# Half-height matmul tiles for the folding and the numerators, constant rows copied by DMA, and a new table of offsets

## The chip, the core and the metric

The kernel runs on one core of a Trainium2 chip. The metric is the time of the whole program on the device, in microseconds (us), as the median of several runs. TensorE (PE) does the matmuls and loads their weights, VectorE (DVE), ScalarE (ACT) and GpSimd (POOL) do the elementwise work, and SyncE (SP) issues all DMAs of this kernel, in order, from one queue.

## What is computed

Two attention layers over 2048 tokens of width 1024, with 32 heads of 32, are computed and set side by side. Layer A is causal softmax attention within four segments plus a compressive memory across them. Layer B is linear attention with a learned feature map. The change touches three places: the constants of A's score product, the product of B's per-head matrix `w_phi` with its projection weights (folding), and B's numerators.

```python
def _B_ref(x, wqkv, w_phi, wo):
    qkv = (x @ wqkv) -> q, k, v of [heads 32, tokens 2048, 32]
    pq = jnp.einsum("bhsd,hdf->bhsf", q, w_phi)      # folded: (wqkv, w_phi) before x
    pk = jnp.einsum("bhsd,hdf->bhsf", k, w_phi)
    phi_q = jnp.concatenate([_softmax(pq), _softmax(-pq)], axis=-1)   # 64 features a head
    phi_k = jnp.concatenate([_softmax(pk), _softmax(-pk)], axis=-1)
    kv = jnp.einsum("bhsf,bhsd->bhfd", phi_k, v)     # 64 x 32 a head
    z = jnp.einsum("bhsf->bhf", phi_k)
    num = jnp.einsum("bhqf,bhfd->bhqd", phi_q, kv)   # the numerators
    den = jnp.einsum("bhqf,bhf->bhq", phi_q, z)[..., None] + 1e-6
    return (num / den -> [tokens, 1024]) @ wo
```

## The kernel before

Nothing is issued in the order in which it is written. The code records operations (`op(engine, duration, function, reads, writes, priority)`) in a graph; `Graph.run` then plays the engines forward with the durations written down for each operation and, whenever an engine is free, issues the ready operation of least priority number. The table `MOVES` adds an offset to the priority, by engine and by the running number of the job (a stretch of operations of equal priority). PSUM has eight banks; `Graph.bank` gives them out by kind (`proj`, `s`, `misc`, `pv`, `kv`), and `KEEP` and `MOST` say how many a kind may hold. Numbers are kept in f32 and multiplied as pairs of f16 halves, three products for each (high by high, high by low, low by high), except in the folding, which is an f32 matmul.

The program has four stages.

- **Start** (to about 20 us). Thirty-two f32 matmuls of an identity (L1195) run on PE while the first weights and the first segment land. ACT measures the sum of the absolute weights (L469), PE spreads it over the partitions (L405), DVE measures the segment (L463), and both are split into halves (L415 to L429). The first product (L394) needs all of that. Tiles `S12` to `S14` (`stk`) hold queries and keys; their partitions 96 to 103 carry a constant that the score product (L971) uses, written by three ACT operations (L651).
- **Layer A** (to about 917 us). For each of 32 units, `produce` makes queries, keys and values and `attend` the scores, exponentials and sums. One `fold` stands in each unit: it loads a 128x512 block of `wqkv` (`st`), multiplies its four 128x128 pieces by a 128x128 matrix that has four heads' `w_phi` on its diagonal (`phib`), L1112, into one `misc` bank, and DVE scales the bank into `quad` (L1115).
- **Layer B, keys and values, then queries** (to about 1531 us). `strassen` (L608) makes the products with `x`. For each of 16 token blocks c and each half hb of the heads, POOL, DVE and ACT make the features and their halves, a DMA transposes them into `pt` (L1603), and the numerators follow (L1612): 24 matmuls, each with a 128x64 weight tile (two heads, their 64x32 matrices on the diagonal, the rest zero) and 128 moving columns, into the 64 upper or the 64 lower partitions of a `pv` bank. ACT (L1616) and DVE (L1618) take the bank into the halves of `ot`, and `project` (L394, `misc<-S,ot`) multiplies by B's output weights.
- **Layer A's output product** (L1666, to the end).

The folding and the numerators are these lines.

```python
for c in range(4):
    op(PE, 0.22, lambda c=c: nc.tensor.matmul(ps()[:, c, :], st()[:, c * 128:(c + 1) * 128], phib()[:, g, :], ...
...
for g in range(4):
    for a, b in ((0, 0), (0, 1), (1, 0)):
        for k in range(2):
            nc.tensor.matmul(pn()[64 * k:64 * k + 64, g, :], kls()[:, a, 8 * hb + 2 * g + k, :], pt()[:, b, 2 * g + k, :], ...
```

Of the kernel before, what the change touches and what calls it, by code (L numbers as in the profile page):

```python
# [12 lines left out]
AF = mybir.ActivationFunctionType  # L13
OP = mybir.AluOpType
# [5 lines left out]
D = 1024  # L20
# [41 lines left out]
    "ACT": {  # L62
# [9 lines left out]
    "POOL": {  # L72
        67: 17, 70: -1, 93: -6, 131: -0.5, 141: 1, 148: -7.5, 199: 13.5, 217: -4, 238: -38, 245: 0.5, 250: -4.5, 312: -5},
    "SP": {
        88: 5.5, 89: 3.5, 134: 33.5, 149: -3.5, 226: -19.5},
# [23 lines left out]
class Graph:  # L99
# [84 lines left out]
    def run(self):  # L184
# [15 lines left out]
        def bank(kind):  # L200
            rest = [x for x in banks if x[1] is None]
            if used[kind] >= self.MOST[kind] or len(rest) <= sum(
                    max(0, n - used[k]) for k, n in self.KEEP.items() if k != kind):
                return never, None
            return min((x[0], i) for i, x in enumerate(banks) if x[1] is None)

        def start(o):
            t = max(o.ready, held["POOL" if o.eng == "DVE" else "DVE"]) if o.port else o.ready
            for b in o.banks:
                if b.at is None:  # L210
                    t = max(t, bank(b.kind)[0])
            return t

        def safe(o):

            return max([o.safe] + [bank(b.kind)[0] + self.SLACK for b in o.banks if b.at is None])

        count = 0
        for _ in self.ops:
# [16 lines left out]
            n = 0  # L236
# [43 lines left out]
def tile_kernel(ctx: ExitStack, tc: tile.TileContext, ax, aw, awv, awo, beta, bx, bwqk, bwv, bphi, bwo, out):  # L280
# [369 lines left out]
    for t in stk:  # L650
        op(ACT, 2.0, lambda t=t: nc.scalar.activation(t()[96:104, 1], sel[96:104, :, None].to_broadcast([8, 4, 512]), AF.Copy),  # L651
           w=[(t, (1, 3))], prio=0.3)
# [420 lines left out]
    def fold(n, prio, dep=()):  # L1073
# [36 lines left out]
        ps = bank("misc", [128, 4, 128], "fold")  # L1110
        for c in range(4):
            op(PE, 0.22, lambda c=c: nc.tensor.matmul(ps()[:, c, :], st()[:, c * 128:(c + 1) * 128], phib()[:, g, :],  # L1112
                                                      start=True, stop=True), r=[st, phib], w=[ps], prio=prio, need=[qd])
        k = 2 * q + hb
        op(DVE, 0.62, lambda: nc.vector.tensor_scalar(qd()[:, k], ps().rearrange("p c n -> p (c n)"), si()[:, 1:2], None, op0=OP.mult),  # L1115
# [622 lines left out]
```

## Time and profile before

| | |
|---|---|
| median of 3 runs | 1698.13 us (1698.09 to 1698.71) |
| profiled execution | 1699.08 us, its span 1697.4 us |
| mean granted TensorE clock | 0.994 of full |
| PE busy | 1668.2 us (98%) |
| DVE, ACT, POOL busy | 1354.2, 1158.9, 965.4 us |

The span is the time from the first to the last instruction; 1.68 us of the profiled execution lie around it. PE is busy nearly throughout, so an engine other than PE matters where PE waits for it, and a microsecond of PE's own work counts in full where PE does not wait. Matmuls are pipelined: a row's duration reaches from the first matmul's start to the last one's end, while the pace is the distance from start to start.

### The profile page before, as it was taken

The page shows a single profiled execution, that of the slowest core. Times are in us where ns is not written, and L with a number is a line of the kernel's source. Part 1 is how long each engine was busy: PE and PEld are TensorE (multiplying, and loading weights), DVE is VectorE, ACT ScalarE, POOL GpSimd, SP SyncE. Part 2 cuts the span into 40 slices and gives each one's busy share as a digit, 9 for nine tenths or more (in the row PEclk, how much of TensorE's full clock was granted, in tenths as well). Part 3 has the DMA queues.
Part 4 walks back from the last instruction along what each step waited for, and adds up shares of the span by engine and source line. Part 5 has one row for each costly group of instructions (what it writes and reads, how often), then busy time and mean ns, then how long its engine had stood idle before and what let it go on. Part 6 is the DMA issues. An engine that isn't in the chain of part 4 may idle for free.

```text
span 1697.4 us, 38668 instructions
## 1 busy us (share of the span) xinstructions
PE 1668.2 (98%) x14408; PEld 1002.5 (59%) x14408; DVE 1354.2 (80%) x3205; ACT 1158.9 (68%) x2131; POOL 965.4 (57%) x1280
## 2 busy tenths in 40 slices
PE   8999999999999999999999999999999999999999
PEld 6677676766767767767765455445544444444444
DVE  5889998899988869698895779677998887975441
ACT  8788899878879797868675477765545644544331
POOL 3346588554468885848552577645488887640000
PEclk8999999999999999999999999999999999999999
DMA  5556465755776665764467465467645876773311
GB/s 192 165 183 176 139 206 175 242 160 163 225 179 204 184 173 150 199 189 131 95 182 266 156 224 162 137 194 278 224 94 149 199 162 174 214 168 129 124 62 62
DMA packets 261933, 292.47 MB, mean 172 GB/s; under 512 B 138865, under 2 KB 192881, under 8 KB 255089
## 3 DMA queue, kind: packets, MB, share of 16 engines
q1 hardware_dynamic: 261744, 290.01, 57.3%
q8 instruction: 113, 1.85, 0.5%
q14 instruction: 76, 0.61, 0.1%
HBM read 161.17 MB, written 86.05 MB: 146 GB/s over the span
## 4 chain that ended last, share of the span: by engine, by line
PE 45%; DVE 5%; DMA 1%; ACT 0%; issue 0%; SPq 0%; DVEq 0%; ACTq 0%
PE proj L608 17%; PE misc L394 8%; PE proj L1666 5%; PE s L608 4%; PE s L1666 2%; PE misc L608 2%; PE kv L1423 1%; PE misc L1666 1%; PE pv L1612 1%; DVE S L1600 1%; PE proj L394 1%; DVE mx L1262 1%; DVE r L1272 1%; DVE dn L1581 1%; PE pv L1007 1%; PE s L971 1%
## 5 line engine op out<-in xcount | busy, mean ns | idle before, releaser
L394 PE MATMUL proj<-S,S 128*128 128x128 f16 (+1 forms) x3072 | 508.8, 301 | 4.1 <-ACT S L427 1.7
L394 PEld LDWEIGHTS <-S 128*128 128x128 f16 x4608 | 330.2, 98 | 152.0 <-issue 13.0
L608 PE MATMUL proj<-S,S 128*128 128x512 f16 x1584 | 364.6, 379 | 2.4 <-ACT cs L614 2.4
L608 PEld LDWEIGHTS <-S 128*128 128x128 f16 x2016 | 191.9, 98 | 220.5 <-issue 3.3
L984 POOL TENSOR_SCALAR_AFFINE_SELECT ph<-ph 128x256 f16<-128x256 f16 (+1 forms) x448 | 195.8, 458 | 155.2 <-DVE ph L978 136.7
L876 DVE CUSTOM_DVE_ANT_0 s<-s,causal 128x512 f32<-128x512 f32 (+3 forms) x512 | 242.9, 509 | 15.2 <-PE s L870 11.5
L978 DVE SCALAR_TENSOR_TENSOR ph<-s,ph 128x512 f16<-128x512 f32 x320 | 210.2, 683 | 36.8 <-ACT ph L977 35.3
L977 ACT ACTIVATE ph<-s 128x512 f16<-128x512 f32 x320 | 189.9, 653 | 1.0 <-PE pv L1007 0.2
L394 PE MATMUL misc<-S,ot 128*128 128x512 f16 x768 | 170.8, 379 | 1.8 <-DVE ot L1618 1.8
L1269 ACT ACTIVATE e<-e,sk 128x256 f32<-128x256 f32 x256 | 113.3, 497 | 63.7 <-DVE e L1266 58.2
L394 PEld LDWEIGHTS <-ot 128*128 128x128 f16 x768 | 73.8, 98 | 90.3 <-DVE ot L1618 2.2
L971 PE MATMUL s<-S 104*128 104x512 f16 (+3 forms) x512 | 114.4, 299 | 1.9 <-ACT S L898 0.8
L870 PE MATMUL s<-S 96*128 96x512 f16 (+3 forms) x512 | 112.8, 299 | 2.1 <-DVE mt L876 1.4
L975 ACT ACTIVATE s<-s,os 128x512 f32<-128x512 f32 x160 | 106.5, 707 | 9.0 <-PE s L971 8.5
L975 ACT ACTIVATE s<-s,bd 128x512 f32<-128x512 f32 x160 | 106.6, 712 | 7.1 <-PE s L971 6.5
L1578 POOL TENSOR_TENSOR e<-e,zb 128x512 f32<-128x512 f32 x64 | 87.2, 1376 | 30.4 <-DVE r L1272 25.6
L394 PE MATMUL proj<-wv,S 128*128 128x128 f16 x1536 | 103.0, 219 | 0.0
L1007 PEld LDWEIGHTS <-ph 128*128 128x128 f16 x2560 | 87.1, 96 | 15.5 <-issue 0.8
L1272 DVE TENSOR_REDUCE r<-e 128x32 f32<-128x1024 f32 x64 | 76.9, 1208 | 24.2 <-ACT e L1269 24.2
L1007 PE MATMUL pv<-vl,ph 128*128 128x66 f16 (+1 forms) x2560 | 91.9, 184 | 0.5 <-DVE h L824 0.3
L876 DVE DVE_READ_ACCUMULATOR2_ANT mt<- 128x1 f32 x512 | 72.4, 141 | 0.0
L1011 DVE TENSOR_REDUCE oall<-pv 128x132 f32<-128x264 f32 x128 | 54.5, 426 | 19.1 <-PE pv L1007 18.5
(334 smaller groups left out, 3268.8 us busy)
## 6 DMA issues: line engine op xcount, KB each, us to landing
S<-xf_d SPq DMA_DIRECT2D x126, 256.0 KB
S<-h SPq DMA_DIRECT2D x192, 128.0 KB
S<-wf_d SPq DMA_DIRECT2D x21, 1024.0 KB
st<-bwqk SPq DMA_DIRECT2D x64, 256.0 KB
out<-os SPq DMA_DIRECT2D x40, 256.0 KB
S<-aw SPq DMA_DIRECT2D x16, 512.0 KB
wa_d<-S SPq DMA_DIRECT2D x16, 512.0 KB
wf_d<-fo SPq DMA_DIRECT2D x32, 256.0 KB
```

The costliest lines, as they stand in the source:

```text
L394: op(PE, dur, lambda c=c, a=a, b=b, lv=lv, rv=rv: nc.tensor.matmul(pv(), lv(), rv(), start=(c == 0 and a + b == 0), stop=(c == n - 1 and a ...
L608: op(PE, 0.215, lambda n=n, a=a, b=b, lv=lv, rv=rv: nc.tensor.matmul(ps(), lv(), rv(), start=(start and n == 0 and a + b == 0), stop=(n == ...
L870: nc.tensor.matmul(ps()[:, o:o + 128 * i + 128], st()[0:96, 0, h, 128 * i:128 * i + 128], st()[0:96, 1, h, 0:128 * i + 128], start=True, s ...
L876: dve(0.12 + 0.00113 * n, lambda h=h, i=i, o=o, n=n: nc.vector.tensor_tensor_reduce(ps()[:, o:o + n], ps()[:, o:o + n], causal[:, 512 - n: ...
L971: nc.tensor.matmul(ps()[:, o:o + n], st()[0:104, 1, h, 128 * j:128 * j + 128], st()[0:104, 0, h, 128 * j:512], start=True, stop=True)
L975: act(0.59, lambda: nc.scalar.activation(ps(), ps(), AF.Exp, bias=0.0, scale=bdv()[:, 3, i2, 0:1]), r=[(bd, i2)], w=[ps])
L977: act(0.5, lambda: nc.scalar.activation(ph()[:, 0], ps(), AF.Copy, scale=2.0 ** 14), r=[ps], w=[(ph, 0)])
L978: dve(0.6, lambda: nc.vector.scalar_tensor_tensor(ph()[:, 1], ps(), 2.0 ** 14, ph()[:, 0], op0=OP.mult, op1=OP.subtract), r=[ps, (ph, 0)], ...
L984: nc.gpsimd.affine_select(pd, pd, pattern=[[0, n], [1, 128]], compare_op=OP.is_ge, fill=0.0, base=0, channel_multiplier=-1)
L1007: nc.tensor.matmul(ps()[:, i, n0:n1], ph()[:, a, o:o + 128], vl()[:, j, h, n0:n1], start=(i == 0 and a == 0), stop=(j == min(i, 2)), skip_ ...
L1269: op(ACT, 0.41, lambda i=i: nc.scalar.activation(e()[:, 4 * i:4 * i + 4], e()[:, 4 * i:4 * i + 4], AF.Exp, bias=0.0, scale=sk()[:, i:i + 1 ...
L1666: op(PE, 0.215, lambda n=n, a=a, b=b: nc.tensor.matmul(ps(), v(a)[:, n, :], wform[w]()[:, b, n, :], start=(start and n == 0 and a + b == 0 ...
```

## The change

**Folding.** Each of the four pieces becomes two matmuls of 64 rows: rows 0 to 63 of `st` by the upper left 64x64 of `phib` into a `misc` bank, rows 64 to 127 by the lower right into a `kv` bank. The array is used as two tiles of 64 rows by 128 columns, the f32 weights are still 128 columns wide, and each matmul moves 64 columns instead of 128. The eight matmuls are one operation of the planner, so nothing comes between them. DVE scales two banks of 256 columns.

**Numerators.** Each head has a matmul of its own: a weight tile of 64 rows by 32 columns, 128 moving columns, 48 instead of 24 for each (c, hb). The array is used as eight tiles (two of rows, four of columns), each eight matmuls in a row go to eight different tiles, and the two row halves go to two banks (`pv` and `kv`) that both halves hb of a block fill. ACT and DVE take each bank once for a block, so both wait for the numerators of both hb. The rows of `bwo` are permuted on the host to match.

**Constant rows.** GpSimd writes those of the first `stk` tile, and two DMAs of SP copy them into the other two. ACT's three operations are gone.

**Order.** `MOVES` is another table (212 offsets, before 131); for it two of its lines stand below. The planner's search for banks takes operations that open two banks.

```diff
     "DVE": {
-        43: -0.5, 70: 1, 85: -12.5, 88: -6, 93: -8, 101: -5.5, 103: 11, 106: -2, 109: 2, 114: -3.5, 118: 3.5, 129: -6, 135: -5,
...
+        4: -1.5, 10: -2.5, 15: -5, 39: -30.5, 43: -22, 45: -24, 51: 4.5, 73: 7.5, 88: -45.5, 89: -51, 93: -44.1, 100: -8.5,
...
     stk = [G.buf("slot", [128, 2, 4, 512], F16, f"S{12 + i}") for i in range(3)]
-    for t in stk:
-        op(ACT, 2.0, lambda t=t: nc.scalar.activation(t()[96:104, 1], sel[96:104, :, None].to_broadcast([8, 4, 512]), AF.Copy),
-           w=[(t, (1, 3))], prio=0.3)
+    op(POOL, 2.6, lambda: nc.gpsimd.tensor_copy(stk[0]()[96:104, 1], sel[96:104, :, None].to_broadcast([8, 4, 512])),
+       w=[(stk[0], (1, 3))], prio=0.3)
+    for t in stk[1:]:
+        op(SP, 0.6, lambda t=t: nc.sync.dma_start(t()[96:104, 1], stk[0]()[96:104, 1]), r=[(stk[0], (1, 3))],
+           w=[(t, (1, 3))], prio=0.3, lat=1.6, kb=32)
...
-        ps = bank("misc", [128, 4, 128], "fold")
-        for c in range(4):
-            op(PE, 0.22, lambda c=c: nc.tensor.matmul(ps()[:, c, :], st()[:, c * 128:(c + 1) * 128], phib()[:, g, :],
-                                                      start=True, stop=True), r=[st, phib], w=[ps], prio=prio, need=[qd])
+        ps = [bank(k, [128, 4, 64], "fold") for k in ("misc", "kv")]
+
+        def f():
+            for c in range(4):
+                for h in range(2):
+                    v = slice(64 * h, 64 * h + 64)
+                    nc.tensor.matmul(ps[h]()[:, c, :], st()[v, c * 128:(c + 1) * 128], phib()[v, g, v], start=True, stop=True)
+
+        op(PE, 0.55, f, r=[st, phib], w=ps, prio=prio, need=[qd])
         k = 2 * q + hb
-        op(DVE, 0.62, lambda: nc.vector.tensor_scalar(qd()[:, k], ps().rearrange("p c n -> p (c n)"), si()[:, 1:2], None, op0=OP.mult),
-           r=[ps, si], w=[(qd, k)], prio=prio)
+        for h in range(2):
+            op(DVE, 0.38, lambda h=h: nc.vector.tensor_scalar(
+                qd()[:, k].rearrange("p (c n) -> p c n", n=128)[:, :, 64 * h:64 * h + 64], ps[h](), si()[:, 1:2], None, op0=OP.mult),
+               r=[ps[h], si], w=[(qd, k)], prio=prio)
...
+        pn = [bank(k, [128, 4, 128], "sums") for k in ("pv", "kv")]
         for hb in range(2):
...
-            pn = bank("pv", [128, 4, 128])
-
             def f(pn=pn, pt=pt, hb=hb):
-                for g in range(4):
+                for n in range(2):
                     for a, b in ((0, 0), (0, 1), (1, 0)):
-                        for k in range(2):
-                            nc.tensor.matmul(pn()[64 * k:64 * k + 64, g, :], kls()[:, a, 8 * hb + 2 * g + k, :], pt()[:, b, 2 * g + k, :],
-                                             start=(a + b == 0), stop=(a == 1), skip_group_check=True)
-
-            op(PE, 0.85, f, r=[(kls, (0, hb)), (kls, (1, hb)), pt], w=[pn], prio=P)
...
+                        for k in range(4):
+                            for h in range(2):
+                                i, rows_ = 4 * n + k, slice(64 * h, 64 * h + 64)
+                                nc.tensor.matmul(pn[h]()[32 * k:32 * k + 32, 2 * hb + n, :],
+                                                 kls()[rows_, a, 8 * hb + i, 32 * h:32 * h + 32], pt()[rows_, b, i, :],
+                                                 start=(a + b == 0), stop=(a == 1), skip_group_check=True)
+
+            op(PE, 0.5, f, r=[(kls, (0, hb)), (kls, (1, hb)), pt], w=pn, prio=P)
+        for h in range(2):
...
+            op(ACT, 0.55, lambda pn=pn, h=h, oh=oh: nc.scalar.activation(oh(0), pn[h](), AF.Copy, scale=2.0 ** -15),
+               r=[pn[h]], w=[(ot, (0, h))], prio=P)
+            op(DVE, 0.62, lambda pn=pn, h=h, oh=oh: nc.vector.scalar_tensor_tensor(
+                oh(1), pn[h](), 2.0 ** -15, oh(0), op0=OP.mult, op1=OP.subtract),
+               r=[pn[h], (ot, (0, h))], w=[(ot, (1, h))], prio=P)
```

Line numbers of the changed kernel are 8 to 23 higher: L469 becomes L477, L394 becomes L402, L1112 becomes L1126.

On ACT, at the start of the program, the constants (`S<-sel`) stand before, ahead of and between the two sums of absolute weights (`wgb<-S`):

```order
L651 ACT_TABLE_LOAD
L651 ACTIVATE S_134<-sel 8x2048
L651 ACTIVATE S_150<-sel 8x2048
L469 ACTIVATE S_161,wgb<-S_140 128x1024
L651 ACTIVATE S_167<-sel 8x2048
L469 ACTIVATE S_161,wgb<-S_140 128x1024
L415 ACTIVATE S_140<-S_140,wgs 128x512 x2
```

and in the changed kernel ACT begins with the sums:

```order
L477 ACT_TABLE_LOAD
L477 ACTIVATE S_159,wgb<-S_138 128x1024 x2
L423 ACTIVATE S_138<-S_138,wgs 128x512 x2
L424 ACTIVATE S_159<-S_138 128x512 x2
L423 ACTIVATE S_138<-S_138,wgs 128x512 x2
```

The constants have moved to POOL (one operation, behind its memsets) and to SP (two DMAs, behind the load of `beta`).

On PE, at the first folding before (L971 is the score product, L1112 the folding):

```order
L971 MATMUL s<-S_134 128x256
L1112 MATMUL misc<-phib,st 128x128 x4
L971 LDWEIGHTS S_134
L971 MATMUL s<-S_134 128x512
L971 LDWEIGHTS S_134
```

and in the changed kernel (L402 is the product of queries and keys, L1126 the folding; the pair of `misc` and `kv` comes four times, of which two stand here):

```order
L402 MATMUL proj<-S_759,S_297 128x512
L1126 MATMUL misc<-phib,st 128x64
L1126 MATMUL kv<-phib,st 128x64
L1126 MATMUL misc<-phib,st 128x64
L1126 MATMUL kv<-phib,st 128x64
```

Before, the 128 pieces stand in 39 groups with other matmuls between them; now they stand in 31 groups of eight or sixteen half-height matmuls.

On PE, at about 60 us, where the second segment's sizes come in (`misc<-...,one` and `<-...,xam` are one- and two-column matmuls, L943 the memory update, L394 the product with the second segment, `S_837`), before:

```order
L971 MATMUL s<-S_134 128x128
L734 MATMUL misc<-wgb,xam 128x2 x2
L772 MATMUL misc<-wvb,xam 128x1
L405 MATMUL misc<-wgb,one 128x1
L943 MATMUL misc<-vf_126,pkt 128x132 x4
L730 MATMUL misc<-pr,one 128x4
L394 LDWEIGHTS S_161
L394 MATMUL proj<-S_837,S_161 128x512
```

and in the changed kernel:

```order
L413 MATMUL misc<-xam,one 128x1
L744 MATMUL misc<-wgb,xam 128x2 x2
L402 LDWEIGHTS S_245
L402 MATMUL proj<-wv,S_245 128x128
L402 LDWEIGHTS S_245
L402 MATMUL proj<-wv,S_245 128x128
L782 MATMUL misc<-wvb,xam 128x1
```

The value products of the first segment (`proj<-wv,S`), which stood ahead of this place, now stand between its small matmuls.

## Rows read from the trace of the kernel before

**Rows 1.** The page, busy time of each engine, its share of the span, instructions.
```profile
PE 1668.2 (98%) x14408; PEld 1002.5 (59%) x14408; DVE 1354.2 (80%) x3205; ACT 1158.9 (68%) x2131; POOL 965.4 (57%) x1280
```

**Rows 2.** Waits of PE over the span: total us, times, longest us.
```profile
PE misc L405 <- ACT S L469: 3.6, 2, 2.1
PE pv L1612 <- DMA pt<-S: 3.0, 3, 1.5
PE misc L394 <- DVE ot L1618: 1.8, 1, 1.8
```

**Rows 3.** Timeline of the start: start us, us, engine, line, what, idle before.
```profile
4.13 3.70 ACT L651 ACTIVATE S<-sel 8x2048 f16<-8x2048 f32 x2 [2.06 <-DVE sel L343]
7.85 1.06 ACT L469 ACTIVATE S<-S 128x1024 f16<-128x1024 f32 x1
...
10.95 1.06 ACT L469 ACTIVATE S<-S 128x1024 f16<-128x1024 f32 x1
...
12.15 0.59 PE L405 MATMUL misc<-wgb,one 128*128 128x1 f32 x2 [1.50 <-ACT S L469]
...
13.05 3.04 DVE L463 TENSOR_REDUCE twb<-S 128x1 f32<-128x512 f32 x5
13.93 4.53 POOL L417 TENSOR_TENSOR S<-S,S 128x512 f16<-128x512 f32 x4 [10.06 <-ACT S L416]
...
19.36 9.36 PE L394 MATMUL proj<-S,S 128*128 128x512 f16 x29 [1.07 <-ACT S L427]
```

**Rows 4.** Windows: PE, PEld, DVE, ACT, POOL busy, clock, DMA share, GB/s.
```profile
0.00:6.00 6.00, 4.37 (x25) 4.37 (x26) 2.83 (x10) 3.16 (x3) 3.17 (x15) 1.00 0.63 223
0.00:11.20 11.20, 6.97 (x44) 6.58 (x44) 4.52 (x15) 8.28 (x7) 3.17 (x15) 1.00 0.81 287
```

**Rows 5.** Timeline of PE around one block's numerators, and its weight loads.
```profile
1282.42 0.25 PE L1612 MATMUL pv<-pt,kls 128*64 128x128 f16 x2
...
1282.78 0.50 PE L1612 MATMUL pv<-pt,kls 128*64 128x128 f16 x11
...
1248.93 0.86 PE L1612 MATMUL pv<-pt,kls 128*64 128x128 f16 x24
1249.73 2.55 PE L394 MATMUL misc<-S,ot 128*128 128x512 f16 x11
...
1281.68 0.81 PE L394 MATMUL misc<-S,ot 128*128 128x512 f16 x3
```

**Rows 6.** Timeline of PE: 128 and 66 or 33 columns on the whole array.
```profile
54.84 3.35 PE L394 MATMUL proj<-wv,S 128*128 128x128 f16 x57
...
77.55 0.72 PE L1007 MATMUL pv<-vl,ph 128*128 128x66 f16 x20
```

**Rows 7.** Windows of the first blocks of B's queries and later; columns as in Rows 4.
```profile
1240.00:1260.00 20.00, 17.84 (x129) 8.37 (x129) 19.96 (x31) 8.51 (x17) 17.92 (x18) 1.00 0.58 119
...
1360.00:1400.00 40.00, 40.00 (x286) 19.13 (x284) 32.70 (x52) 20.59 (x38) 35.22 (x35) 1.00 0.69 161
```

**Rows 8.** Timeline of PE at a folding; its scaling (ns min/median/max, first and last start).
```profile
76.66 1.05 PE L1112 MATMUL misc<-phib,st 128*128 128x128 f32 x8
...
L1115 DVE TENSOR_SCALAR quad<-misc,sif x32: 735/745/752, 72.4 to 841.7; 128x512 f32<-128x512 f32 x32
```

**Rows 9.** Timeline of two f32 weight loads for one-column matmuls; that line's loads.
```profile
200.06 0.30 PEld L530 LDWEIGHTS misc<-tops,one 128*128 128x128 f32 x2
...
200.31 0.38 PE L394 MATMUL proj<-S,S 128*128 128x512 f16 x1
...
L530 PEld LDWEIGHTS misc<-tops,one x16: 185/190/192, 200.1 to 1033.5; 128*128 128x128 f32 x16
```

**Rows 10.** Timeline of PE at the second segment's first product, and a window there.
```profile
63.11 1.01 PE L394 MATMUL proj<-S,S 128*128 128x512 f16 x2 [0.88 <-DVE ph L978]
...
65.21 4.00 PE L394 MATMUL proj<-S,S 128*128 128x512 f16 x9 [0.87 <-DVE S L429]
...
65.00:70.00 5.00, 4.79 (x14) 2.11 (x14) 3.80 (x10) 4.67 (x8) 3.33 (x5) 0.53 0.26 95
```

More of the change, by code (lines that the diff above doesn't have):

```diff
@@ L58 @@
     "DVE": {
[3 rows of a table removed]
[8 rows of a table added]
     "ACT": {
[3 rows of a table removed]
[4 rows of a table added]
     "PE": {
[5 rows of a table removed]
[7 rows of a table added]
     "POOL": {
-        67: 17, 70: -1, 93: -6, 131: -0.5, 141: 1, 148: -7.5, 199: 13.5, 217: -4, 238: -38, 245: 0.5, 250: -4.5, 312: -5},
-    "SP": {
-        88: 5.5, 89: 3.5, 134: 33.5, 149: -3.5, 226: -19.5},
+        63: -32.5, 126: -0.5, 128: -5.5, 154: -13.5, 169: -0.5, 173: 5, 199: 7.5, 221: 0.5, 225: -10.5, 234: -8.5, 240: 2,
+        245: 0.5, 250: -1, 252: -0.7, 254: 0.5, 257: -2, 312: -9.5, 326: -8, 376: 4, 389: -3},
 }
@@ L198, in run, with bank, opening @@
                 lists[o.eng].append(o)
-        def bank(kind):
-            rest = [x for x in banks if x[1] is None]
+        def bank(kind, before=()):
+            rest = sorted(x[0] for x in banks if x[1] is None)[len(before):]
             if used[kind] >= self.MOST[kind] or len(rest) <= sum(
-                    max(0, n - used[k]) for k, n in self.KEEP.items() if k != kind):
-                return never, None
-            return min((x[0], i) for i, x in enumerate(banks) if x[1] is None)
+                    max(0, n - used[k] - (k in before)) for k, n in self.KEEP.items() if k != kind):
+                return never
+            return rest[0]
+        def opening(o):
+            kinds = [b.kind for b in o.banks if b.at is None]
+            return [bank(k, kinds[:i]) for i, k in enumerate(kinds)]
         def start(o):
             t = max(o.ready, held["POOL" if o.eng == "DVE" else "DVE"]) if o.port else o.ready
[L209 to L212, printed above, removed]
+            return max([t] + opening(o))
         def safe(o):
-            return max([o.safe] + [bank(b.kind)[0] + self.SLACK for b in o.banks if b.at is None])
+            return max([o.safe] + [t + self.SLACK for t in opening(o)])
         count = 0
@@ L1615, in tile_kernel @@
-            op(PE, 0.85, f, r=[(kls, (0, hb)), (kls, (1, hb)), pt], w=[pn], prio=P)
-            op(ACT, 0.55, lambda pn=pn, hb=hb, otv=otv: nc.scalar.activation(
-                otv()[:, 0, 4 * hb:4 * hb + 4, :], pn(), AF.Copy, scale=2.0 ** -15), r=[pn], w=[(ot, (0, hb))], prio=P)
-            op(DVE, 0.62, lambda pn=pn, hb=hb, otv=otv: nc.vector.scalar_tensor_tensor(
-                otv()[:, 1, 4 * hb:4 * hb + 4, :], pn(), 2.0 ** -15, otv()[:, 0, 4 * hb:4 * hb + 4, :], op0=OP.mult, op1=OP.subtract),
-               r=[pn, (ot, (0, hb))], w=[(ot, (1, hb))], prio=P)
+                        for k in range(4):
[4 more added lines that the diff above has]
+                                                 start=(a + b == 0), stop=(a == 1), skip_group_check=True)
@@ new lines, in tile_kernel, with oh @@
+            op(PE, 0.5, f, r=[(kls, (0, hb)), (kls, (1, hb)), pt], w=pn, prio=P)
+        for h in range(2):
+            def oh(a, h=h, otv=otv):
+                return otv()[:, a].rearrange("p (g h) t -> p h g t", h=2)[:, h]
+            op(ACT, 0.55, lambda pn=pn, h=h, oh=oh: nc.scalar.activation(oh(0), pn[h](), AF.Copy, scale=2.0 ** -15),
[3 more added lines that the diff above has]
+               r=[pn[h], (ot, (0, h))], w=[(ot, (1, h))], prio=P)
@@ L1727 @@
         "bphi": np.ascontiguousarray(np.asarray(B_w_phi)),
-        "bwo": rows(B_wo),
+        "bwo": rows(np.asarray(B_wo).reshape(4, 4, 2, 32, D).transpose(0, 2, 1, 3, 4).reshape(D, D)),
     }
```

28 rows, old and new, of the table MOVES are left out of this document.

## The prediction

> **What bounds the kernel now.** I read the page's busy times first: PE is busy for 1668.2 of 1697.4 us [rows 1]. Then the list of PE's waits: it is short, and only three places matter here, the sums of weights at the start (3.6 us in two waits), the transposes ahead of the numerators (3.0) and one project that waits for `ot` (1.8) [rows 2]. So PE's own pace decides, and I price each edit by the distance from matmul start to matmul start in the timeline, since durations overlap. Last come the windows, for the stretches in which PE is not the bound: where B's queries begin, DVE is busy for 19.96 of 20 us and PE for 17.84; later PE is full and DVE at 82% [rows 7].
>
> **The start: ACT's constants.** Two constants end at 7.83 us (4.13 + 3.70), the first sum begins at 7.85; the second sum begins at 10.95, behind the third constant; PE waits for both [rows 2, 3]. Their weights, two DMAs of 0.52 MB that were issued first, can be no reason: 6 us at 223 GB/s are 1.34 MB [rows 4]. Without the constants ACT can sum at once, and PE has its sixteen warm-up matmuls until then. I take both of PE's waits as gone, **-3.6 us**. What is late next is the segment: weights and segment together are 3.15 MB, and 11.2 us at 287 GB/s are 3.21 MB [rows 4]; one more DVE sum of 0.61 us (five in 3.04) ends at 11.8, where the last one ended at 16.09 [rows 3]. So DVE allows 4.3 us, and 3.6 is not cut off. What was added is hidden: POOL is idle for 10.06 us ahead of its first subtraction [rows 3], and an operation that took ACT 1.9 us fits there even if POOL needs three times that; on SP the two small DMAs wait for it, with the loads of `phib` and of the second segment behind them, which are used only after the first product. Bounds: 0 (PE's clock is at half there anyway and the earlier matmuls run slow) to -5 (the segment decides alone).
>
> **The numerators.** Before, from the first of 24 to the next product takes 1249.73 - 1248.93 = 0.80 us [rows 5]. Eleven of them take 0.50, one about 0.22, so a pair advances by (0.50 - 0.22)/5 = 0.056 us; two start together (0.25 for both). One matmul of 128 columns on the whole array also advances by 0.056 ((3.35 - 0.22)/56) [rows 6], so the two column tiles do run side by side. Eleven steps are 0.62; 0.18 is the way out. The way in: of three products in 0.81, the last starts at 1282.11, and the first numerator at 1282.42 [rows 5], 0.31 later instead of 0.215, so 0.095. Together 0.895 a group. After: 48 matmuls in six sets of eight tiles. If eight tiles run side by side as two do, that is five steps of 0.056, 0.03 until the eighth has started, and the same ways in and out, 0.585; it saves 0.31, 9.9 us over 32 groups. Eight of these groups lie before 1300 us, where DVE is the bound [rows 7], and DVE's work is not less: there a shorter PE only waits longer. So 24 x 0.31, **-7.4 us**; bounds 0 (row halves one after the other: twelve steps, as now) to -9.9.
>
> **The folding.** Before, eight records (each f32 matmul leaves two) take 77.55 - 76.66 = 0.89 us, 0.111 each [rows 6, 8]. Two things pace at 0.111, and the change shortens only one of them. The matmul moves 128 columns and will move 64. But the weights stay 128 columns of f32, and their load alone has that length: of two loads that take 0.30 us together and 0.19 each, the second starts 0.11 after the first, although its matmul moves a single column; and the next f16 product starts at 200.31, another 0.11 on [rows 9]. With half the rows there are twice as many loads, sixteen. I assume that the loads of the two row halves go side by side, since two column tiles do; within a piece the two records of one half follow each other, so the pairs are shifted by one: eight steps of 0.111 from first to last, 0.89. The array changes its tiles, so the ways in and out (0.095 + 0.18) come on top: 1.165 instead of 0.89, and 32 x 0.275 less one group that stands with another is **+8.5 us**. Bounds: -5.4 if the moving columns pace (eight steps of 0.056 + 0.275 = 0.72), +37 if loads go one by one (sixteen steps, 2.05). I take the value nearest to the row with one moving column, as that is the only row that separates the two paces. The Trainium skill speaks for the load: TensorE: Matmul & The Clock Gate, LDWEIGHTS (loading the stationary operand), says that the time of a load goes by its columns and that 32 rows take as long as 128. Against it TensorEngine Tiling (Array Packing), Theoretical Speedup, gives up to twice the speed where a dimension is 64 or less; by that the folding would be the -5.4. No run here shows a load of 64 rows.
>
> DVE scales two banks instead of one, each of half the columns; at 745 ns for 512 columns [rows 8] that is between 0 and 0.2 us more a folding, and PE does not wait for it.
>
> **The order.** One place can be priced. Near 63 us PE waits 0.88 and 0.87 us, and then runs at half clock: nine products take 4.00 us, (4.00 - 0.38)/8 = 0.45 each instead of 0.215, and the granted clock is 0.53 over the 5 us [rows 10]. The waits are 1.75 and the clock about 0.47 x 5 = 2.35. The new order puts ready value products among the small matmuls there, so that PE has work while DVE and ACT split the second segment. I take half of the 4.1 as gone, **-2.1 us**; bounds -4 to +4, since the same table moves hundreds of other instructions whose waits the order does not tell.
>
> **Sum.** -3.6 - 7.4 + 8.5 - 2.1 = -4.6. The profiled execution took 1699.1 (1697.4 and 1.7 around it), so 1694.5 for such an execution; the median of the runs lies 0.95 below it, so **1693.5 us**.
>
> **Rivals.**
> - *The moving columns pace the folding.* For it: the matmul's 128 columns take 0.111 too, so the row at the folding alone cannot tell which it is. Against it: the loads with one moving column. It gives -5.4 in place of +8.5: 1679.6.
> - *Half-height loads go one by one.* For it: no row shows two row tiles. It gives +37 instead of +8.5: 1722. This is the slower side; it decides as soon as a folding takes more than 1.3 us instead of 0.89, since then the other terms (-13.1) are eaten.
> - *The eight tiles of the numerators do not overlap.* Small matmuls on one array, 66 and 33 columns in turn, advance by (0.72 - 0.19)/19 = 0.028 [rows 6]; 47 such steps and 0.275 are 1.6 us, +0.70 a group, +22 instead of -7.4: 1723. The Trainium skill has such a floor, about 25 ns from start to start however few the columns (TensorE: Matmul & The Clock Gate, Wait — 56ns, not 53.3ns?). Against it: two numerators start within 0.01 [rows 5], so the step holds within a tile, not between tiles.
> - *The blocks wait for `ot`.* Both banks now fill only with the second half hb, so ACT's and DVE's two operations each come at once behind it, where DVE is full [rows 7]. If four of the first blocks then wait as the one with 1.8 us does [rows 2], that is +7: 1700.5. Against it: PE has products of the next queries to do meanwhile.
>
> **How the numbers follow.** Chances: forecast 0.45, moving columns 0.30, `ot` 0.12, loads one by one 0.08, no overlap 0.05. About 0.2%, 3.4 us, is what a measurement can tell from no change, so faster means under 1694.7, slower above 1701.5. The forecast's own range is 1688 to 1701 by the bounds of the start and the order; of its 0.45 I count 0.26 as faster, 0.13 as the same, 0.06 as slower. The moving columns add 0.30 to faster, `ot` 0.06 to each of the others, the last two 0.13 to slower: 0.56, 0.19, 0.25. The range goes from 1671 (moving columns, with the bounds of start and order) to 1705 (`ot` with the order's bound); outside are the two cases near 1722 and a little of the tails, under 2 in 10.
>
> **What would show it.** The folding: sixteen records, start to next product near 1.16 us (0.72 if the columns pace, 2.0 if loads queue). The numerators: 48 matmuls, first to next product near 0.49, and in the windows near 1240 us PE no busier than now. The start: the first product at about 15.8 us instead of 19.36, and no wait of L413 for ACT. The place near 63 us: a clock above 0.53. The forecast is wrong if the folding falls below its present 0.89, or if PE's waits in A grow by more than the 4 us I allow.

## The result and the profile after

The changed kernel took 1702.2 us (median of 13 runs) against 1696.8 for the kernel before (also of 13): a ratio of 1.0029, 95% interval 1.0022 to 1.0036, so about 5 us slower. It lies inside the predicted range and on the wrong side of zero. The profiled execution has a span of 1700.7 us. The trace kept of the kernel before is of a run of 1699.1 us, 2.3 above its median, so below the traces are compared by their rows and not by their spans.

PE is busy for 2.5 us less than in [rows 1], with a thousand matmuls more; DVE has 11 us more. The waits of PE, in the form of [rows 2]:

```profile
PE 1665.7 (98%) x15432; PEld 993.7 (58%) x15432; DVE 1365.5 (80%) x3237; ACT 1158.0 (68%) x2128; POOL 971.8 (57%) x1281
```
```profile
PE pv L1630 <- DVE kls L1489: 5.9, 1, 5.9
PE pv L1630 <- DMA pt<-S: 5.6, 4, 2.1
PE misc L906 <- DVE mh L901: 4.1, 5, 2.3
...
PE misc L413 <- ACT S L477: 0.2, 1, 0.2
PE misc L402 <- DVE ot L1641: 0.2, 1, 0.2
```

The waits for ACT's sums at the start are down from 3.6 us to 0.2, and the one for `ot` from 1.8 to 0.2. A wait of 5.9 us has come for the low halves of the numerators' weights (`kls`, the sums over B's keys), the transposes take 5.6 instead of 3.0, and `mh` (row maxima in layer A) takes 4.1.

The start, as [rows 3] showed it: PE's first product stands at 15.31 us instead of 19.36.

```profile
13.63 0.38 PE L413 MATMUL misc<-xam,one 128*128 128x1 f32 x2 [1.73 <-DVE xam L481]
...
15.31 0.59 PE L402 MATMUL proj<-S,S 128*128 128x512 f16 x2 [1.07 <-ACT S L435]
```

A folding: on PE the first two and the last of its eight pairs, then the third and fourth pair of its weight loads ([rows 8, 9] are the rows of before):

```profile
80.67 0.59 PE L402 MATMUL proj<-S,S 128*128 128x512 f16 x2
81.19 0.32 PE L1126 MATMUL misc<-phib,st 64*128 64x64 f32 x1
81.20 0.32 PE L1126 MATMUL kv<-phib,st 64*128 64x64 f32 x1
81.35 0.27 PE L1126 MATMUL misc<-phib,st 64*128 64x64 f32 x1
81.36 0.27 PE L1126 MATMUL kv<-phib,st 64*128 64x64 f32 x1
...
82.02 0.27 PE L1126 MATMUL misc<-phib,st 64*128 64x64 f32 x1
82.03 0.27 PE L1126 MATMUL kv<-phib,st 64*128 64x64 f32 x1
82.23 0.39 PE L402 MATMUL proj<-S,S 128*128 128x512 f16 x1
```
```profile
81.41 0.19 PEld L1126 LDWEIGHTS misc<-phib,st 64*128 64x128 f32 x1
81.41 0.19 PEld L1126 LDWEIGHTS kv<-phib,st 64*128 64x128 f32 x1
81.52 0.19 PEld L1126 LDWEIGHTS misc<-phib,st 64*128 64x128 f32 x1
81.53 0.19 PEld L1126 LDWEIGHTS kv<-phib,st 64*128 64x128 f32 x1
```

Two loads of 64 rows start together, each takes the 0.19 us of 128 rows, and the next pair follows 0.11 later. From the first record to the next product are 1.04 us instead of 0.89, and the way in is 0.09 longer: 0.24 a folding.

The numerators of one half of a block, first, second and last of 48 records and the next product, against [rows 5]:

```profile
1292.18 0.23 PE L1630 MATMUL pv<-pt,kls 64*32 64x128 f16 x1
1292.18 0.23 PE L1630 MATMUL kv<-pt,kls 64*32 64x128 f16 x1
...
1292.56 0.22 PE L1630 MATMUL kv<-pt,kls 64*32 64x128 f16 x1
1292.71 0.39 PE L402 MATMUL misc<-S,ot 128*128 128x512 f16 x1
```

0.53 us from first to next product instead of 0.80. Last the windows: the place near 63 us, then the one that answers to the first of [rows 7].

```profile
62.00:70.00 8.00, 8.00 (x81) 4.55 (x80) 5.66 (x10) 8.00 (x17) 3.03 (x8) 1.00 0.01 2
```
```profile
1240.00:1260.00 20.00, 10.93 (x132) 4.85 (x131) 20.00 (x25) 6.94 (x14) 14.60 (x15) 0.74 0.39 79
```

Near 63 us PE is full at the full clock (in [rows 10] it had a clock of 0.53 there). At 1240 us it has lost 6.9 us of busy time against before, while DVE is full to the last hundredth.

### The profile page after: what moved, and what is told of

The parts are those of the page before. It is cut to its first block, busy times and chain, and to the rows that moved or that the text cites. A ratio compares the mean times of both kernels' runs of the same rounds, so it can differ in the third digit from the quotient of the medians.

```text
span 1700.7 us, 40765 instructions
## 1 busy us (share of the span) xinstructions
PE 1665.7 (98%) x15432; PEld 993.7 (58%) x15432; DVE 1365.5 (80%) x3237; ACT 1158.0 (68%) x2128; POOL 971.8 (57%) x1281
## 4 chain that ended last, share of the span: by engine, by line
PE 75%; DVE 13%; ACT 5%; DMA 3%; issue 2%; POOL 1%; SPq 0%; DVEq 0%; ACTq 0%; POOLq 0%
PE proj L402 21%; PE proj L616 16%; PE misc L402 9%; PE proj L1689 5%; PE s L981 3%; PE pv L1017 3%; DVE s L886 3%; PE s L616 3%; PE s L880 3%; PE s L1689 2%; DVE ph L988 1%; PE misc L616 1%; PE misc L1689 1%; PE misc L1126 1%; ACT ph L987 1%
## 5 line engine op out<-in xcount | busy, mean ns | idle before, releaser
L402 PE MATMUL proj<-S,S 128*128 128x512 f16 (+1 forms) x3072 | 503.2, 300 | 2.3 <-ACT S L435 1.1
L402 PEld LDWEIGHTS <-S 128*128 128x128 f16 x4608 | 328.8, 98 | 150.0 <-issue 6.7
L616 PE MATMUL proj<-S,S 128*128 128x512 f16 x1584 | 369.1, 381 | 2.0 <-ACT cs L622 2.0
L886 DVE CUSTOM_DVE_ANT_0 s<-s,causal 128x256 f32<-128x256 f32 (+3 forms) x512 | 243.0, 509 | 14.8 <-PE s L880 10.9
L402 PE MATMUL misc<-S,ot 128*128 128x512 f16 x768 | 172.9, 382 | 0.2 <-DVE ot L1641 0.2
L402 PEld LDWEIGHTS <-ot 128*128 128x128 f16 x768 | 74.0, 98 | 89.4 <-issue 2.3
L402 PE MATMUL proj<-wv,S 128*128 128x128 f16 x1536 | 103.8, 219 | 0.0
L1618 DVE TENSOR_TENSOR S<-e,S 128x512 f16<-128x512 f32 x64 | 71.8, 1167 | 5.4 <-ACT S L1616 5.1
```

Source lines behind the costliest of these rows:

```text
L402: op(PE, dur, lambda c=c, a=a, b=b, lv=lv, rv=rv: nc.tensor.matmul(pv(), lv(), rv(), start=(c == 0 and a + b == 0), stop=(c == n - 1 and a ...
L616: op(PE, 0.215, lambda n=n, a=a, b=b, lv=lv, rv=rv: nc.tensor.matmul(ps(), lv(), rv(), start=(start and n == 0 and a + b == 0), stop=(n == ...
L886: dve(0.12 + 0.00113 * n, lambda h=h, i=i, o=o, n=n: nc.vector.tensor_tensor_reduce(ps()[:, o:o + n], ps()[:, o:o + n], causal[:, 512 - n: ...
```

## Experiments

All times are ratios to the kernel before, run on the same chip in turn; 0.1% is 1.7 us. The runs were made on three chips, so two runs are compared by their ratios, and the bounds given in us come from both intervals.

### The table by itself

Three kernels undo or apply a part in the source and let the planner order the rest anew. `e2_old_table` puts before's `MOVES` into the changed kernel, `e3_new_table` does the reverse, `e1_fold_back` takes back the folding's code, `e7_start_numer` adds constants and numerators to the kernel before.

> The changed kernel with the folding as it was (whole rows, one bank, 128 columns moved), and all else, its table too, left. If the folding costs what its records say (31 groups of which each is about 0.24 us longer, 7.6 us in all) and PE has no slack at those places, this kernel is 7.6 us under the changed one: some 1694.6 with 1702.2 for the changed one and 1696.8 for the kernel before, a ratio to before of about 0.9987. If the folding lies beside waits of PE on other engines, it comes out at 1700 to 1702.

> The changed kernel with the offsets of the kernel before; constants, numerators and folding stay as changed. Theory: the new table put the second half's k sums late on VectorE and has PE wait for them, 7.4 us more idle of PE behind the first product; then the idle falls back to about 19 us and the time to about 1695 (ratio to before 0.997 to 1.000). Rival: the waits come from the shape of the numerators (one group for both halves, VectorE full beside them), whatever the table; then it stays at 1700 to 1703, and the waits near 1255 us stay in its trace. Third: the new table was made for the new jobs, and without it the time is worse than the changed kernel's, over 1704.

> The kernel before with the offsets of the changed one and no other edit. If the table carries the loss of 7.4 us by itself, it takes 1701 to 1706 (ratio 1.002 to 1.005), with the wait for the k sums near 1255 us in its trace; if the waits come from the numerators, it is within 2 us of before. If the table only suits the new jobs, it is over 1706.

> The kernel before with two of the four parts: constants written by GpSimd and copied by two DMAs, and the numerators in row tiles (with the two banks of the planner and the reordered output weights); the folding and the table stay as before, but for one offset of PE (job 282) that would leave the planner without a bank. If start and numerators are worth what their records say (4.0 and 8.5 us) and the table is what lost time, it takes about 1685 to 1689 (ratio 0.993 to 0.995). If the numerators bring waits that eat them, 1692 to 1696.

Measured: e1 1.0102 (1.0088 to 1.0116), e2 1.0419 (1.0399 to 1.0440), e3 1.0271 (1.0253 to 1.0290), e7 1.0311 (1.0297 to 1.0326). All are much slower than either kernel. The longest waits of e2 and of e3 show how a table fails that was made for other jobs:

```profile
PE pv L1623 <- DMA pt<-S: 23.5, 6, 17.9
```
```profile
PE pv L1619 <- DVE kls L1479: 12.6, 1, 12.6
```

What follows is the third case named for e2 and e3: a table belongs to its jobs, and these four runs tell nothing on a single edit. In the next ones the planner sees unchanged jobs, and only what a step emits is edited; the order of all other instructions is the same, row by row.

### One part undone, the order kept

`f1_fold`, in the changed kernel (two products to each bank; DVE scales 256 columns of a bank):

```
-                for h in range(2):
-                    v = slice(64 * h, 64 * h + 64)
-                    nc.tensor.matmul(ps[h]()[:, c, :], st()[v, c * 128:(c + 1) * 128], phib()[v, g, v], ...)
+                nc.tensor.matmul(ps[c // 2]()...[:, c % 2, :], st()[:, c * 128:(c + 1) * 128], phib()[:, g, :], ...)
```

> The changed kernel in its own order, in which only the inside of the folding's two steps is as before: four products of whole rows and 128 columns, two to each of its two banks, and VectorE takes a bank as 256 columns. The planner sees the same jobs, so every other instruction stands where it stood. If the folding lengthens the path by what its records show, it is 7.6 us under the changed kernel: 1694.6 against 1702.2 (ratio to before 0.9987). If it lies beside waits, 1700 to 1702.

Measured 1.0003 (0.9994 to 1.0012), 0.26% or 4.4 us under the changed kernel. So the folding does lose time. By the records it is 31 times 0.24 = 7.4 us shorter; 4.4 (2.5 to 6.3) arrive. In the traces PE idles for 13.4 us from 100 to 917 us in f1 and for 11.4 in the changed kernel, so part of the gain goes into waits.

`f2_numer` (24 matmuls of the kernel before into the two banks, old order of the output weights):

```
+                            nc.tensor.matmul(pn[g % 2]()[64 * k:64 * k + 64, 2 * hb + g // 2, :],
+                                             kls()[:, a, 8 * hb + 2 * g + k, :], pt()[:, b, 2 * g + k, :], ...)
```

> The changed kernel in its own order, in which only the matmuls inside the numerators' step are those of before (whole rows, 64 columns each, output weights in the old order), into the same two banks. If the numerators' gain of 8.5 us reached the end, this takes 1710.7; if PE spends part of the gain waiting for VectorE and for the transposes in the stage from 1246 us, the difference is smaller: 6 us if the 8 groups ahead of 1300 us are bound by VectorE, 0 to 2 us if the waits eat all of it.

Measured 1.0061 (1.0048 to 1.0074), 0.32% or 5.4 us over the changed kernel. The step itself is 0.26 us shorter in each of 32 groups, 8.3 us; 5.4 (2.9 to 7.9) arrive.

`f5_all_back` undoes both and writes the constants by ACT, in the changed kernel's places:

> The changed kernel's order with none of its three edits in the instructions: folding and numerators as in the kernel before, the three constants written by ScalarE in the places of the GpSimd copy and the two DMAs. What is left against the kernel before is the order of the instructions (table, and the two banks of a pair). Theory: the order is worth +10 us (5.4 measured, less -4.0, -8.5 and +7.6), so about 1707 (ratio 1.006). Rival: the order costs nothing and a term was mis-sized; then 1695 to 1699.

Measured 1.0057 (1.0045 to 1.0069). With before's matmuls and with the constants on ACT, the changed kernel's order costs 9.7 us (7.6 to 11.7). More than the table is in this: a folding still takes two banks and two scalings on DVE (64 in all, 30.4 us, where before has 32 that take 23.9), the evictions still wait for both halves of a block, and of ACT's constants one stands ahead of the sums and two behind them (the first product is at 18.13 us). No run separates these from the table. Two places show what the order does. From 100 to 400 us PE idles for 8.2 us instead of 3.2 (the kernel before, then f5); why it does is not pinned down:

```profile
100.00:400.00 300.00, 296.75 (x3229) 209.77 (x3228) 273.65 (x781) 268.26 (x482) 195.41 (x304) 1.00 0.58 184
```
```profile
100.00:400.00 300.00, 291.80 (x3120) 207.02 (x3118) 272.99 (x798) 257.29 (x465) 186.89 (x285) 0.99 0.60 183
```

The other is from 1215 to 1262 us. DVE's splittings and scalings there with the window, in the kernel before and then in f5 (count, busy us, mean ns):

```profile
L1600 DVE TENSOR_TENSOR S<-e,S 128x512 f16<-128x512 f32 x8 | 9.5, 1252 | 0.0
L1467 DVE TENSOR_TENSOR ez<-ez,zs 128x512 f32<-128x512 f32 x1 | 0.7, 686 | 0.0
L1472 DVE TENSOR_TENSOR kls<-ez,kls 128x512 f16<-128x512 f32 x1 | 0.7, 685 | 0.0
...
1215.00:1262.00 47.00, 43.07 (x263) 20.43 (x262) 46.57 (x82) 22.81 (x47) 34.80 (x36) 1.00 0.54 158
```
```profile
L1618 DVE TENSOR_TENSOR S<-e,S 128x512 f16<-128x512 f32 x8 | 12.2, 1583 | 0.0
L1489 DVE TENSOR_TENSOR kls<-ez,kls 128x512 f16<-128x512 f32 x1 | 2.1, 2078 | 0.0
L1484 DVE TENSOR_TENSOR ez<-ez,zs 128x512 f32<-128x512 f32 x1 | 1.7, 1748 | 0.0
...
1215.00:1262.00 47.00, 38.07 (x219) 18.30 (x218) 47.00 (x78) 18.25 (x37) 33.61 (x35) 0.89 0.47 144
```

The same ten operations take 16.0 us instead of 10.9. In the kernel before six of them take 0.68 to 0.73 us and four 1.45 to 2.4; in f5 eight take 1.6 to 2.4. By the timeline, each of the long ones begins while a GpSimd instruction on two tensors runs (`e` by `zb` and `e` by `r` above all). The new order makes more of them meet one, and DVE, which has no slack (47.00 of 47 us), has 5.1 us more to do. PE loses 5.0 us of busy time in this window, and its clock falls to 0.89 of full speed; up to 1300 us it wins some of that back (74.40 us busy from 1215 on, against 77.24). How the 9.7 us divide between the two places, single executions cannot tell.

### The edits in the order of before

`g1_start` and `g2_start_numer` keep the plan of the kernel before. For the second bank of each half, g2 takes one that the plan leaves free, and evicts two times 256 columns:

```
+            more = G.fixed(None)
+            more.make = lambda more=more: pools["psum"].tile([128, 4, 128], F32, name="more", tag=f"bank{more.at}", bufs=1)
...
+                for h in range(2):
+                    nc.scalar.activation(half(0, h), two[h]()[:, 0:2], AF.Copy, scale=2.0 ** -15)
```

> The kernel before in its own order with the constants alone changed (GpSimd writes one, two DMAs copy it). The first product starts 4 us earlier; if nothing between there and the end gives it back, 1692 to 1693 (ratio 0.9975); if the load of ScalarE or the transfers are late afterwards anyway, 1695 to 1697.

> The kernel before in its own order (its plan is kept, only what a step emits is changed): constants by one GpSimd copy and two DMAs, and the numerators in row tiles, each half with a second bank that the plan left free, so each half's two evictions are two of 256 columns. If the edits are good and only the changed kernel's order is bad, 4.0 and 8.5 us less, and a little more for 32 more instructions on ScalarE and on VectorE: 1684 to 1689 (ratio 0.993 to 0.995). If the shorter numerators only wait for VectorE in the stage from 1245 us: 1690 to 1693.

g1: 0.9986 (0.9978 to 0.9995), 2.4 us faster than before, and the only version that leaves nothing out and beats both kernels clearly. Its first product stands at 15.21 us, 4.2 earlier; 2.4 of it (0.8 to 3.7) are seen at the end. g2: 1.0005 (0.9996 to 1.0015), so the numerators do not gain here, they lose what the start won. PE's waits of g2 from 1225 us on:

```profile
PE misc L412 <- DVE ot L1655: 6.2, 3, 3.3
PE pv L1640 <- DMA pt<-S: 3.4, 4, 1.5
PE more L1640 <- DVE ot L1655: 2.1, 1, 2.1
```

Before had 1.8 us for `ot` [rows 2]; the shorter numerators, with twice as many evictions, wait for DVE. Which of the two, shorter matmuls or more evictions, makes the wait is not separated.

### Whose waits are they

`a1_sums_early` moves seven instructions of the changed kernel (list of: instruction, neighbour, before or behind it), `a2_copy_early` one more; `h1_fold_sums` and `h2_fold_copy` are the same with before's folding.

```
+        return ((t["scaled", 1], t["scaled", 0], 1), (t["high", 1], t["high", 0], 1), (t["low", 1], t["low", 0], 1),
+                (t["out", 0, 0], t["part", 1, 0, 0], 0), (t["out", 0, 1], t["part", 1, 0, 0], 0),
+                (t["copy", 0, 0], t["whole", 1, 0, 0], 0), (t["copy", 0, 1], t["whole", 1, 0, 0], 0))
```

> The changed kernel with all its edits and its order, but for seven instructions near 1223 to 1259 us: the scaling and the low part of the k sums' second half on VectorE, with ScalarE's copy between them, stand right behind those of the first half, and the two evictions of the first block's numerators (ScalarE's and VectorE's) ahead of the next block's splitting. Theory: PE's wait of 5.9 us for the k sums and the half clock behind it are the order's largest single loss, and go: 4 to 8 us less than the changed kernel's 1702.2, so 1694 to 1698 (ratio 0.998 to 1.001). Rival: VectorE is full there (20.00 of 20 us), so the wait only moves to what now comes later; then 1700 to 1702.

> The same seven moves together with the folding of the kernel before (as in f1_fold, 1695.9). If both effects add, 1688 to 1692 (ratio 0.995 to 0.998), faster than both kernels; by the rival 1694 to 1696.

> a1_sums_early and one move more: ScalarE's copy of the score bank (cs) near 1267 us, which PE waited for 6.3 us and which stood behind an exponential that waited for VectorE, goes ahead of that exponential. If single instructions stand wrongly, PE's 6.3 us fall to 1 or 2 and the time by 4 to 5 us under a1 (1702.4), to 1697 or 1698. If VectorE's load sets the pace, PE waits for the next thing of VectorE and the time stays at 1700 to 1703.

> The same with the folding of the kernel before (h1_fold_sums took 1696.8): 1691 to 1693 if the wait goes, 1695 to 1697 if VectorE's load sets the pace.

Measured: a1 1.0037 (1.0026 to 1.0048), h1 1.0006 (0.9998 to 1.0015), a2 1.0036 (1.0024 to 1.0048), h2 0.9993 (0.9984 to 1.0001). None differs by more than the intervals from the kernel without the moves (the changed kernel 1.0029, f1 1.0003): the side of the rival in each expectation. PE's longest wait from 1225 to 1300 us, in a1 and then in a2 (in the changed kernel it was the 5.9 us for `kls`; `cs` is ACT's copy of a product's bank):

```profile
PE proj L654 <- ACT cs L660: 6.3, 1, 6.3
```
```profile
PE pv L1673 <- DVE e L1321: 4.0, 1, 4.0
```

The wait for `kls` is gone in a1, and one of 6.3 us for `cs` has come; with `cs` moved, one of 4.0 for DVE's `e`. The name in the list of waits is that of the last link; in both cases the chain leads back to DVE. In a1's timeline of ACT, `cs` stands behind an exponential that waited 7.62 us for DVE:

```profile
1266.70 0.51 ACT L1324 ACTIVATE e<-e,sk 128x256 f32<-128x256 f32 x1 [7.62 <-DVE e L1321]
1267.11 0.58 ACT L660 ACTIVATE cs<-proj 128x512 f32<-128x512 f32 x1
```

### Less work for DVE

```
-                    hv()[:, 1, 512 * q:512 * q + 512], ev(e)[:, 512 * q:512 * q + 512], ...
+                n = 512 if c == 0 else 16
...
+                    hv()[:, 1, 512 * q:512 * q + n], ev(e)[:, 512 * q:512 * q + n], ...
```

> The changed kernel in its own order; VectorE's splitting of the weighted queries (60 of its 64 subtractions of 512 columns, the blocks after the first) does 16 columns instead of 512, so the low halves of those blocks are left out. It takes some 65 us from VectorE behind 1250 us. If VectorE's load makes the waits of the stage, PE's idle time there falls from 12.3 to about 6 us (the first block's waits stay) and the time to 1692 to 1696; if not, it stays near 1702.

> d1_less_vector with the matmuls of the numerators as in the kernel before (f2_numer with the same work left out of VectorE). If VectorE ate a part of the numerators' gain, this is now the whole 8 to 9 us over d1_less_vector; if the gain was never larger, it stays 5 us over it.

d1: 1.0002 (0.9994 to 1.0011), 4.6 us under the changed kernel; d2: 1.0052 (1.0037 to 1.0067). Between them lie 0.50%, 8.5 us, where the changed kernel and f2 differ by 5.4. The window from 1262 to 1530 us of the changed kernel, f2, d1 and d2, in this order:

```profile
1262.00:1530.00 268.00, 263.69 (x2518) 121.54 (x2517) 230.70 (x372) 139.78 (x269) 195.93 (x206) 0.99 0.70 170
```
```profile
1262.00:1530.00 268.00, 266.64 (x1812) 126.89 (x1811) 224.87 (x366) 137.51 (x266) 196.31 (x205) 1.00 0.66 168
```
```profile
1262.00:1530.00 268.00, 268.00 (x2594) 124.31 (x2593) 190.65 (x367) 139.68 (x271) 183.26 (x205) 1.00 0.69 173
```
```profile
1262.00:1530.00 268.00, 268.00 (x1799) 127.55 (x1798) 191.07 (x363) 135.01 (x262) 184.41 (x206) 1.00 0.68 168
```

With DVE relieved of 40 us PE does not wait once in this window, with either form of the numerators, and the runs differ by 8.5 us, near the 8.3 of their records. With DVE's full work PE idles for 4.3 us with the short numerators and for 1.4 with the long ones. The intervals of the two differences (8.5, give or take 3.0, and 5.4, give or take 2.5) overlap, so the times do not show that the gain grows; the windows show that DVE's load makes the waits that eat a part of it. With the long numerators the relief brings no clear gain (d2 is 1.5 us under f2, give or take 3.4), so DVE's work behind 1262 us is not shown to be a part of what the order costs. The wait for `kls` at 1249 us stays in d1 (5.7 us), as expected, since the first block's work is all there; d1 does not test DVE's load at that place.

### The pace of the folding

`e6_half_columns`, in the kernel before:

```
-            nc.tensor.matmul(ps()[:, c, :], st()[:, c * 128:(c + 1) * 128], phib()[:, g, :], ...)
+            nc.tensor.matmul(ps()[:, c, 0:64], st()[:, c * 128:(c + 1) * 128], phib()[:, g, 0:64], ...)
```

> The kernel before, whose folding moves only 64 of its 128 columns against the same full weights of 128 rows and 128 columns; VectorE puts the 64 results twice, so half of the folded weights is left out. Theory: the weight load paces it, a fold stays at 0.89 us and the time within 1 us of before (1695 to 1697). Rival: the moving columns pace it, a fold takes some 0.45 us and the time falls by up to 14 us (1682).

Measured 0.9988 (0.9978 to 0.9998), 2 us less, not 14. A folding with 64 moving columns and the matmul behind it:

```profile
74.31 1.00 PE L1112 MATMUL misc<-phib,st 128*128 128x64 f32 x8
75.14 0.72 PE L1007 MATMUL pv<-vl,ph 128*128 128x66 f16 x20
```

0.83 us for eight records instead of 0.89: the step stays at 0.11, and only the last record ends earlier. Together with the loads for one moving column [rows 9], this shows that the weight load paces it.

## Why the prediction was wrong

**The order: the step that failed.** It was forecast at -2.1 with bounds of 4 either way; f5 measures +9.7 (7.6 to 11.7), with the pairs of banks that go with the order. The one place that was priced came out as said: near 63 us PE is full, at the full clock. Its price was read from one execution, though, and a dear one. Here are 62 to 70 us in the trace of before and in e6's, whose order is the same:

```profile
62.00:70.00 8.00, 6.24 (x21) 2.77 (x21) 6.55 (x17) 7.67 (x15) 5.19 (x10) 0.57 0.21 67
```
```profile
62.00:70.00 8.00, 6.61 (x34) 3.47 (x33) 7.33 (x19) 7.34 (x16) 4.78 (x9) 0.79 0.23 69
```

What failed was to take one place, priced because before's trace shows a stall there, for the whole table, and to bound the rest by that place's size. A new table can make stalls where before has none, and before's trace cannot show them. Two facts at hand pointed there: DVE was busy for 19.96 of 20 us where B's queries begin [rows 7], and the list of instructions shows the second half's `kls` on DVE moved from ahead of the first four splitting subtractions to far behind them. With a full DVE, that was a term of its own: here are DVE's `kls` of before and of after, the latter with the GpSimd instruction that it meets, and a window of after in which PE waits for it and has half its clock (1.2 of 2.4 GHz):

```profile
1227.69 0.69 DVE L1472 TENSOR_TENSOR kls<-ez,kls 128x512 f16<-128x512 f32 x1
```
```profile
1252.59 1.91 POOL L1609 TENSOR_TENSOR e<-e,r 128x1024 f32<-128x1024 f32 x1
1252.98 2.07 DVE L1489 TENSOR_TENSOR kls<-ez,kls 128x512 f16<-128x512 f32 x1
...
1249.30:1259.30 10.00, 4.20 (x41) 1.71 (x42) 10.00 (x14) 3.53 (x7) 8.65 (x10) 0.50 0.00 1
```

a1 showed that this wait, taken alone, is not the price: with it moved away, the time stays and PE waits for the next name. That DVE's backlog is the price at this place is argued from a2's waits and from f5's ten operations; no run took work from DVE there. The idle time from 100 to 400 us stays open.

**The numerators: right in mechanism, a little too large by the records.** From first to next product it falls from 0.80 to 0.53 us (forecast 0.49); the eight tiles do run side by side. 8.3 us of records, forecast 9.9; 7.4 were to arrive, 5.4 did, with bounds (2.9 to 7.9) that still hold the forecast. The reason given for the cut, that a shorter PE only waits longer where DVE is full, was the right one, but it was put on eight groups ahead of 1300 us. The windows of d1 and d2 show waits of this kind in the whole stage, where DVE is busy for 231 of 268 us: not full on average, and still late at single blocks. A window with 82% of DVE busy [rows 7] was read as slack.

**The folding: right in mechanism, half as large at the end.** The load paces, the two row halves load side by side, and the ways in and out come on top. With its way in a folding takes 1.13 us (forecast 1.165), 7.4 us in all by the records instead of 8.5, and 4.4 (2.5 to 6.3) reach the end. That a longer PE step would count in full was wrong here, as f1's longer waits show. The pairs are not shifted by one step either: the records alternate `misc`, `kv`. Of the two sections of the Trainium skill that the prediction set against each other, the trace agrees with TensorE: Matmul & The Clock Gate, LDWEIGHTS (loading the stationary operand): a load of 64 rows takes the same 0.19 us as one of 128. The up to twofold speed of the Trainium skill's TensorEngine Tiling (Array Packing), Theoretical Speedup, does not come here, where the load, not the moving columns, is the limit: a folding takes 1.13 us instead of 0.89.

**The start: right.** The first product is 4.05 us earlier (forecast 3.6). In g1 2.4 us of it reach the end, and the bounds (0.8 to 3.7) just hold the forecast, so that it is smaller at the end is not shown.

**The sum.** The terms as measured are -2.4 - 5.4 + 4.4 + 9.7 = +6.3, and the change as a whole measured +4.9, which is within their intervals. Against the forecast of -4.6 that is 10.9 more: 11.8 from the order, 2.0 from the numerators, 1.2 from the start, and 4.1 less from the folding.

**The range and the signs.** That 1702.2 lies in the stated range is luck: the upper end was set by the rival of `ot`, which did not come, and the forecast's own range ended at 1701. Nor do the ranges follow from their bounds: those of the start and the order put the forecast at 1690 to 1703, not 1688 to 1701. And neither of the two signs of a wrong forecast came. The folding did not get shorter, and PE's idle time in A (20 to 917 us) grew from 9.8 to 11.9 us only, against before's trace, since places like the one near 63 us gave some of it back; from 1215 to 1300 us, which no sign watched, it grew from 7.8 to 11.1.

**The rivals.** Moving columns, loads one by one and tiles without overlap are all excluded by the rows above. The blocks that wait for `ot` came nearest: it named DVE's fullness as what takes the gain, but at another buffer; `ot` itself costs 0.2 us after the change.

## What to carry to other kernels

A table of offsets that a planner reads is part of the code it was tuned with: swapped by itself it cost 46 us (e3 over before) and 66 us (e2 over the changed kernel) here, so price an edit with the order held fixed, by letting the planner see the old job and changing only what it emits. When a change brings a new order, look first at the engine that is full in some window, and follow in the list of instructions what was moved behind what on that engine; do not bound such a term by the stall that it removes. And when a wait moves on to the next name each time one is taken away, look at the engine behind all the names: try what taking work from it does, as d1 did, before reordering again.

## What the runs showed of the hardware

DVE's subtraction of 512 columns takes 0.63 us at the least and 2.46 at the most in the changed kernel; the 15 of the 64 that have no GpSimd instruction beside them take 0.68 to 0.69. Another 38 begin while a GpSimd `tensor_tensor` runs, and 37 of them end 0.55 to 0.57 us behind its end, as the `kls` above does (1255.05 behind 1254.50); the last one ends so behind the next GpSimd instruction. No run took GpSimd's work away, so this is read from the timeline. Shortening the subtraction to 16 columns does not free DVE in proportion: from 1262 to 1540 us the mean falls from 1.12 to 0.41 us only (the changed kernel, twice, and d1).

```profile
L1618 DVE TENSOR_TENSOR S<-e,S x64: 628/738/2462, 1238.7 to 1527.4; 128x512 f16<-128x512 f32 x64
...
L1618 DVE TENSOR_TENSOR S<-e,S 128x512 f16<-128x512 f32 x57 | 61.3, 1117 | 5.4 <-ACT S L1616 5.1
```
```profile
L1619 DVE TENSOR_TENSOR S<-e,S 128x16 f16<-128x16 f32 x56 | 21.4, 409 | 13.4 <-ACT S L1616 13.4
```

So the order decides not only when DVE works but how long it takes: the same ten instructions cost 10.9 us in one order and 16.0 in the other.
